# Attention and MLP on one core: two tiles in one QK tree, a new tile order, LayerNorm 1 on two engines, transposes from SBUF

## The chip, the cores and the metric

The kernel runs on one core of a Trainium2 chip. The metric is the device time of one execution, in microseconds (us). The times of the kernel before are 365.12, 364.94 and 365.55 us, median 365.12. The engines named below are PE (TensorE, the matrix unit, with PEld for its weight loads), DVE (VectorE), ACT (ScalarE), POOL (GpSimd) and SP (SyncE, which here only issues DMAs).

## The reference, cut to what matters

```python
def _A_ref(x, wqkv, wo):                 # 32 heads of width 18, window 8, dilation 2
    q, k, v = split(x @ wqkv)            # D = 576, S = 2048
    idx = pos[:, None] - (arange(8) * 2)[None, :]          # the token itself and 7 earlier ones
    logits = einsum("bhsd,bhswd->bhsw", q, k[idx]) * 18 ** -0.5   # -1e9 where idx < 0
    return einsum("bhsw,bhswd->bhsd", softmax(logits), v[idx]) @ wo

def _B_ref(x, w1, b1, w2, b2):           # hidden width 4608
    return gelu(layernorm(x) @ w1 + b1) @ w2 + b2

h = x + _A_ref(layernorm(x), wqkv, wo)   # LayerNorm 1
out = h + _B_ref(layernorm(h), w1, b1, w2, b2)   # LayerNorm 2 (two layernorms in a row)
```

## The kernel before, in words

Token 16p + j lies in partition p of tile j, so there are 16 tiles of 128 tokens by 576 columns. A query tile j attends to the eight tiles of its own parity. Tiles above j are needed shifted down by one partition: once such a tile's own attention is done, a shifted copy (a "halo") is read back over it from DRAM (`store_halo`, `halo`). Hence tiles attend from high to low: 14, 12, 10, ..., 0, then 15, 13, ..., 1, in pairs called groups (`GROUPS`).

The program is one order of instructions for each engine, written out by hand; nothing is rescheduled. Every queue is served in that order, and SP's too: a DMA that must wait holds all behind it. It has these stages.

- **QKV.** 24 visits (numbered 0 to 23 here) of two "duos". A duo is one tile times one of Wq, Wk, Wv: 18 matmuls of half the array (10 in a first phase, 8 in a second), accumulated in one of three rotating PSUM pairs. ACT copies each result out (`qkv_duo`, its `evac`, L312). The lists `after`, `between` and `hooks` say what is put behind, between and inside the visits. The even tiles (0, 2, 4, ... first) fill visits 0 to 11, the odd ones 12 to 23, each pair of odd tiles taking three.
- **LayerNorm 1** feeds QKV. The mean and variance of nearly all tiles come from DVE (`bn_stats`, L149). Even tiles are centred by DVE, transposed on PE (`tr_x`), copied out of PSUM, and the factor 1/deviation is applied by ACT at the eviction. Odd tiles are normalized by ACT (L175), stored to DRAM (`out_x`) and read back by a transposing DMA in pairs (`in_x`).
- **Attention.** For one tile, DVE multiplies the keys of all eight window places with q (`att_qk_a`, L342), sums 18 head columns in a tree (`att_qk_add`, L348, L355), takes the maximum (`att_max`); ACT does the exponential; DVE divides (`att_den`), multiplies with v (`att_pv_a`, L394) and sums (`att_pv_b`, L400, L401). The result is transposed: for the first two tiles on PE (`tr_o`), for the others by a store to DRAM (`dma_out`, two DMAs) and a transposing DMA (`oT`). Then 18 matmuls with Wo (`wo_duo`), and h = that + x (`ln2_h`).
- **LayerNorm 2** mostly runs on ACT (`ln2_act`, `ln2_send`, L475 to L483, L175) with the power on POOL (L478); its result goes the same way through DRAM and a transposing DMA into `hnT`. Tiles 14 and 12 take statistics on DVE and are transposed on PE (`tr_h`).
- **MLP**, for each of the eight groups, k = 0 to 7. The first half (`mlp1`) is 324 half-array matmuls with hnT as the moving operand and ends in GELUs on ACT (L557), the second (`mlp2`, or `mlp2_fast` from k = 2 on, with fewer products and DVE sums of their operands) ends in the output. In k = 0 and 1 the second half is two tiles of 36 rows each, a row being two matmuls. `ia[n]` hangs work in front of row n of the first tile, `ib[n]` of the second; `m1[v]` in front of visit v of `mlp1`. While group k is in the MLP, DVE does the attention of the next ones; the Wo matmuls and LayerNorm 2 of group k+1 come inside the second half of group k, so that its hnT is there for the next `mlp1`.

The semaphores of SP's DMAs are reused in turn by eight, so that a DMA waits for the eighth before it.

Of the kernel before, what the change touches and what calls it, by code (L numbers as in the profile page):

```python
# [8 lines left out]
ACT = mybir.ActivationFunctionType  # L9
# [8 lines left out]
def kernel(  # L18
# [49 lines left out]
    w2a_sb = wpool.tile([P, FA, D], BF16, name="w2a_sb")  # L68
# [22 lines left out]
    wqh_sb = qp.tile([P, 3, HALF], BF16, name="wqh_sb")  # L91

# [19 lines left out]
    def load_wqkv(t, k0=0, k1=KF):  # L112
        load(wq_sb[:, k0:k1, t * D:(t + 1) * D],
             A_wqkv[k0 * P:k1 * P, t * D:(t + 1) * D].rearrange("(k p) c -> p k c", p=P))

    def load_wqkv_half(engine, t, r):
        c0 = t * D + r * HALF
        engine.dma_start(out=wqh_sb[half_rows(r), t, :], in_=A_wqkv[KF * P:D, c0:c0 + HALF])

    def load_wo(qs):  # L120
        src = A_wo.rearrange("(h d) c -> h d c", h=H)
        for q in qs:
            load(wo_sb[q * H:(q + 1) * H, :, :], src[:, q:4 * KF:4, :])
            load(woh_sb[q * H:(q + 1) * H, :], src[:, 4 * KF + q % 2, q // 2 * HALF:(q // 2 + 1) * HALF])

    def load_w1h():
        load(b1_bf[:], B_b1.rearrange("(ft p) -> ft p", p=P))
        src = B_w1[KF * P:D, :].rearrange("p (u g c) -> p u g c", u=NU, g=2)
# [3 lines left out]
    def load_w1(c):  # L132
        cols = slice(c * F // 6, (c + 1) * F // 6)
        load(w1_sb[:, :, cols], B_w1[0:KF * P, cols].rearrange("(k p) c -> p k c", p=P))
# [7 lines left out]
    def ln_stats(srcs, tag, c1, c0, bufs, first=None, eps=True):  # L142
        n = len(srcs)
        pool = qp if tag.startswith("ln1") else sb
        stats = pool.tile([P, n, 2, nc.vector.BN_STATS_DIM], F32, tag=f"{tag}_stats", name=f"{tag}_stats", bufs=bufs)
        mv = pool.tile([P, n, nc.vector.BN_AGGR_DIM], F32, tag=f"{tag}_mv", name=f"{tag}_mv", bufs=bufs)
        for i, src in enumerate(srcs):
# [3 lines left out]
            if i == 0 and first is not None:  # L151
                first()
        if not eps:
            return mv, None
# [23 lines left out]
    def transpose_in(pt, src, tail=None):  # L178
        for kt in range(KT):
            c = min(kt * P, D - P)  # L180
            if kt < KF or tail is None:
                nc.tensor.transpose(pt[:, kt, :], src[:, c:c + P], ident[:])  # L182
        if tail is not None:
            nc.tensor.transpose(pt[:, KF, :], tail[:].rearrange("p r c -> p (r c)"), ident[:])
            return
        nc.tensor.transpose(pt[0:HP, KF, :], src[:, KF * P:D], ident[:])


    stored = [None]

    def dma_out(src):
        td = dram.tile([P, KT * P], BF16, tag="td", name="td", bufs=4)
        nc.sync.dma_start(out=td[:, 0:D], in_=src)
        stored[0] = nc.sync.dma_start(out=td[:, D:KT * P], in_=src[:, KF * P:D]).ins
        return td

    def dma_transpose(dst, src):
        td = dma_out(src)
        nc.sync.dma_start_transpose(out=dst, in_=td[:])
# [9 lines left out]

    def phase(duo, swap, after):  # L210
        first = last = None
        n = len(duo["g"][0])
        for i in range(n):
            for kt in range(KF if swap else KT):
                for r in range(2):
                    lhsT, rhs = duo["op"](r ^ swap, i, half_rows(r), kt)
# [36 lines left out]
    xnT, xn_tail = {}, {}  # L253
# [7 lines left out]
    def tr_x(js, tag):  # L261
# [12 lines left out]
        for copy in copies:  # L274
            copy()
# [817 lines left out]
```

## Time and profile before

| | |
|---|---|
| times | 365.12, 364.94, 365.55 us |
| span of the profiled execution | 364.9 us (no separate time of that execution is given; the times lie 0.0 to 0.7 above the span) |
| granted TensorE clock | 1.000 |
| first matmul of QKV | 6.26 us |
| first matmul of `mlp1` in k = 0, k = 1 | 71.05 us, 109.22 us |
| end of the first half of k = 5, k = 6 | 273.93 us (256.14 + 17.79), 310.10 us (292.31 + 17.79) |
| PE busy in 39.69-71.05, 71.05-109.22, 109.22-147.03 us | 31.36 of 31.36, 38.17 of 38.17, 37.81 of 37.81 us |
| DVE busy in the same stretches | 28.71, 35.98, 35.63 us |
| PE busy in 147.03 us to the end | 214.12 of 217.9 us |

Busy time of an engine only counts where that engine is the last to be waited for. The chain that ended last and the waits tell that; the timeline gives the order on one engine, with the duration of one instruction and what it had waited for. For DMAs, SP's line gives the time its queue needs to issue one, and "to landing" the time from the start of the issue until the data are there.

### The profile page before, as it was taken

The page shows a single profiled execution, that of the slowest core. Times are in us where ns is not written, and L with a number is a line of the kernel's source. Part 1 is how long each engine was busy: PE and PEld are TensorE (multiplying, and loading weights), DVE is VectorE, ACT ScalarE, POOL GpSimd, SP SyncE. Part 2 cuts the span into 40 slices and gives each one's busy share as a digit, 9 for nine tenths or more (in the row PEclk, how much of TensorE's full clock was granted, in tenths as well). Part 3 has the DMA queues.
Part 4 walks back from the last instruction along what each step waited for, and adds up shares of the span by engine and source line. Part 5 has one row for each costly group of instructions (what it writes and reads, how often), then busy time and mean ns, then how long its engine had stood idle before and what let it go on. Part 6 is the DMA issues. An engine that isn't in the chain of part 4 may idle for free.

```text
span 364.9 us, 11410 instructions
## 1 busy us (share of the span) xinstructions
PE 357.1 (98%) x4891; PEld 291.4 (80%) x4891; DVE 302.3 (83%) x422; ACT 229.2 (63%) x507; POOL 37.1 (10%) x47
## 2 busy tenths in 40 slices
PE   8999799999999999999999999999999999999996
PEld 5678687788778878887888778877887788778874
DVE  5899989999899998999899989998799999710431
ACT  4779655799555684468646954695469366805630
POOL 2141003000111020101010211020101100100000
PEclk9999999999999999999999999999999999999999
DMA  7979998984436743531353155503642342120001
GB/s 226 300 153 330 239 238 184 359 286 73 136 103 88 178 178 77 82 110 51 85 121 88 37 131 91 87 35 92 131 64 59 74 84 72 37 56 19 2 2 33
DMA packets 61907, 43.70 MB, mean 120 GB/s; under 512 B 31888, under 2 KB 60176, under 8 KB 61856
## 3 DMA queue, kind: packets, MB, share of 16 engines
q1 hardware_dynamic: 59968, 41.13, 42.2%
q0 software_dynamic: 1728, 1.77, 4.6%
q8 instruction: 38, 0.62, 0.7%
q10 hardware_dynamic: 160, 0.07, 0.1%
q14 instruction: 13, 0.11, 0.1%
HBM read 21.10 MB, written 12.42 MB: 92 GB/s over the span
## 4 chain that ended last, share of the span: by engine, by line
PE 92%; DMA 5%; SPq 1%; ACT 1%; issue 0%; DVE 0%
PE pm L217 38%; PE po L664 26%; PE pq L217 12%; PE po L576 10%; PE pw L217 5%; DMA oT<-td 2%; DMA wq_sb<-in_A_wqkv_dram 1%; DMA xnT<-xd 1%; DMA xd<-q_all 1%; SPq L104 1%; PE xt_pt L182 1%; ACT kv_ring L312 0%; PE h_pt L182 0%; PE o_pt L182 0%; ACT q_all L175 0%
## 5 line engine op out<-in xcount | busy, mean ns | idle before, releaser
L557 ACT ACTIVATE h_all<-pm,b_sb 128x256 f16<-128x256 f32 (+1 forms) x288 | 108.5, 497 | 69.7 <-PE pm L217 69.7
L217 PE MATMUL pm<-hnT,w_sb 64*128 64x256 bf16 x2304 | 143.0, 269 | 0.0
L217 PEld LDWEIGHTS <-w_sb 64*128 64x128 bf16 x2304 | 111.8, 94 | 15.0 <-issue 1.7
L664 PEld LDWEIGHTS <-h_all 128*128 128x128 f16 x512 | 49.4, 98 | 14.0 <-issue 1.6
L217 PE MATMUL pq<-wq_sb,xnT 64*128 64x288 bf16 x768 | 54.7, 283 | 3.1 <-DMA xnT<-xd 2.2
L217 PEld LDWEIGHTS <-xnT 64*128 64x128 bf16 x864 | 43.1, 94 | 13.0 <-DMA xnT<-xd 2.5
L348 DVE TENSOR_TENSOR prod<-prod 128x2304 bf16<-128x2304 bf16 (+1 forms) x64 | 44.2, 691 | 2.0
L394 DVE TENSOR_TENSOR prod<-kv_ring,probs 128x4608 bf16<-128x4608 bf16 x16 | 40.9, 2555 | 2.4 <-DMA kv_ring<-kv_dram 2.0
L342 DVE TENSOR_TENSOR prod<-kv_ring,q_all 128x4608 bf16<-128x4608 bf16 x16 | 40.8, 2549 | 0.5 <-DMA kv_ring<-kv_dram 0.3
L217 PE MATMUL pm<-hnT,w1h_sb 64*128 64x256 bf16 x288 | 39.2, 269 | 0.0
L664 PE MATMUL po<-w2a_sb,h_all 128*128 128x288 bf16 (+1 forms) x282 | 38.9, 286 | 0.0
L400 DVE TENSOR_TENSOR prod<-prod 128x2304 bf16<-128x2304 bf16 (+1 forms) x32 | 33.9, 1058 | 1.1
L576 PEld LDWEIGHTS <-h_all 128*128 128x128 bf16 x288 | 27.9, 98 | 7.9 <-issue 1.0
L664 PEld LDWEIGHTS <-kv_ring 128*128 128x128 f16 x252 | 24.6, 98 | 6.3
L478 POOL TENSOR_TENSOR ln_rstd<-ln_var,mhalf 128x1 f32<-128x1 f32 x13 | 12.0, 924 | 171.1 <-ACT ln_var L477 171.1
L576 PE MATMUL po<-w2a_sb,h_all 128*128 128x288 bf16 x224 | 28.5, 286 | 0.0
L664 PE MATMUL po<-w2b_sb,h_all 128*128 128x288 bf16 (+1 forms) x142 | 21.3, 286 | 0.0
L217 PE MATMUL pw<-wo_sb,oT 64*128 64x288 bf16 x256 | 19.6, 283 | 0.4 <-DMA oT<-td 0.4
L735 ACT COPY po<-po 128x288 f32<-128x288 f32 x18 | 6.9, 384 | 19.7 <-PE po L664 18.6
L644 DVE TENSOR_TENSOR kv_ring<-h_all 128x1536 f16<-128x1536 f16 (+3 forms) x9 | 6.8, 752 | 14.7 <-ACT h_all L557 14.7
L162 POOL TENSOR_TENSOR ln_rstd<-ln_veps,mhalf 128x1 f32<-128x1 f32 (+2 forms) x14 | 13.4, 967 | 50.3 <-DVE ln_veps L156 34.7
L217 PEld LDWEIGHTS <-oT 64*128 64x128 bf16 x288 | 13.6, 94 | 5.0 <-DMA oT<-td 1.2
(110 smaller groups left out, 387.3 us busy)
## 6 DMA issues: line engine op xcount, KB each, us to landing
w_sb<-in_B_w_dram SPq DMA_DIRECT2D x6, 768.0 KB, 5.9
kv_ring<-kv_dram SPq DMA_DIRECT2D x28, 144.0 KB, 2.8
w2a_sb<-in_B_w_dram SPq DMA_DIRECT2D x4, 1008.0 KB, 6.2
kv_dram<-kv_ring SPq DMA_DIRECT2D x13, 288.0 KB, 3.3
out_dram<-o_sb SPq DMA_DIRECT2D x15, 144.0 KB, 2.6
td<-q_all SPq DMA_DIRECT2D x14, 144.0 KB, 1.8
td<-hn SPq DMA_DIRECT2D x14, 144.0 KB, 1.8
x_all<-in_A_x_dram SPq DMA_DIRECT2D x12, 144.0 KB, 2.9
```

The costliest lines, as they stand in the source:

```text
L162: nc.gpsimd.tensor_tensor(out=rstd[:], in0=veps[:], in1=mhalf[:].to_broadcast([P, n]), op=ALU.pow)
L217: last = nc.tensor.matmul(duo["g"][r ^ swap][i], lhsT=lhsT, rhs=rhs, start=(swap == 0 and i == 0 and kt == 0), stop=(swap == 1 and kt == K ...
L342: nc.vector.tensor_tensor(out=prod[:], in0=k_ring[j % 2], in1=q_all[:, j, :].unsqueeze(1) .to_broadcast([P, W, D]), op=ALU.mult)
L348: nc.vector.tensor_tensor(out=prod[:, :, o * H:o * H + n], in0=prod[:, :, a * H:a * H + n], in1=prod[:, :, c * H:c * H + n], op=ALU.add)
L394: nc.vector.tensor_tensor(out=prod[:].rearrange("p w (d h) -> p w d h", h=H), in0=v_ring[j % 2].rearrange("p w (d h) -> p w d h", h=H), in ...
L400: nc.vector.tensor_tensor(out=prod[:, 0:n, :], in0=prod[:, 0:n, :], in1=prod[:, n:2 * n, :], op=ALU.add)
L478: nc.gpsimd.tensor_tensor(out=rstd[:], in0=var[:], in1=mhalf[:], op=ALU.pow)
L557: pace[0] = nc.scalar.activation(out=hT(grp)[:, f, 0:N], in_=ps[:, r, i * N:(i + 1) * N], func=ACT.Gelu_apprx_tanh, bias=b1_sb[:, f:f + 1] ...
L576: nc.tensor.matmul(banks[half], lhsT=hT(grp)[:, f, i * P:(i + 1) * P], rhs=w2_rows(f)[:, half * HALF:(half + 1) * HALF], start=(f == 0), s ...
L644: nc.vector.tensor_tensor(out=s_slot(t, m0, m1), in0=a, in1=b, op=alu)
L664: nc.tensor.matmul(bank, lhsT=l, rhs=r, start=start, stop=stop, skip_group_check=True)
L735: nc.scalar.copy(out=bank[seed[step][1]], in_=bank[seed[step][0]])
```

## The change

What it does, part by part:

1. **Tile order.** QKV begins with tiles 14 and 12, the first that attend (`LN_ORDER`, called T: 14, 12, 0, 2, 4, 6, 8, 10, 1, 3, ...). The visits are now: 0 k of 14, 12; 1 k of 0, 2; 2 q of 14, 12; 3 k of 4, 6; 4 k of 8, 10; 5, 6 q of 0, 2, 4, 6; 7 to 10 v of all even tiles; 11 q of 8, 10; 12 to 23 as before. Wv is loaded later, Wk is loaded with all its parts on SP's queue.
2. **LayerNorm 1.** Nine tiles take their statistics on DVE (`ln_dve`), seven on ACT (`ln_mean`, `ln_sq`). All are centred on DVE into 640 columns (two runs of 320 that overlap), and all get 1/deviation at the eviction; POOL computes it for two or four tiles at a time (`ln_rstds`).
3. **Transposes.** Only the first four tiles of LayerNorm 1 are transposed on PE, five transposes a tile instead of six. All else is transposed by DMA directly from SBUF to SBUF: LayerNorm 1 tile by tile (`in_x`), attention output and LayerNorm 2 in one DMA for a pair of tiles (`tr_o`, `ln2_in`, tile `y`, one buffer). The stores to DRAM ahead of the transposes are gone. hnT and oT hold the pair as two tiles side by side, so the moving operand of `mlp1` is two runs of 128 columns instead of one of 256.
4. **QK.** For the first four groups of tiles (14 and 12, 10 and 8, 6 and 4, 2 and 0) the products of two tiles are summed once each (`qk_sum9`) into one array and then share one tree (`qk_tree`). For 14 and 12 the sums of PV are shared too (`pv_mul`, `pv_tree`).
5. **Order around the first groups.** Tile 12 reads its window one place lower in the ring (`kv_low`, `window`), so it does not wait for tile 14's halo to overwrite it. The Wo matmuls of 14 and 12 come together behind visit 19, their LayerNorm 2 is on DVE for both (`first_h`, `first_hn`) and by one DMA transpose. In k = 0 both Wo visits of the next group stand in front of row 22 of the second half; the exponential of tiles 10 and 8 is taken together.

The diff, cut:

```diff
+    LN_ORDER = ATT_ORDER[:2] + EVEN[:-2] + ODD
-    def dma_transpose(dst, src):
-        td = dma_out(src)
-        nc.sync.dma_start_transpose(out=dst, in_=td[:])
+    def dma_transpose(dst, src):
+        return nc.sync.dma_start_transpose(out=dst, in_=src).ins
+    def y_transpose(dst, kind, g):
+        return dma_transpose(dst.rearrange("p i k t -> p (i k) t"), y_of.pop((kind, g))[:].rearrange("p i c -> p (i c)"))
+    def in_x(*js):
+        for j in js:
+            if j not in xnT:
+                new_xnT([j, LN_ORDER[LN_ORDER.index(j) + 1]])
+            dma_transpose(xnT[j], x_wide(j))
...
-                scale = dict(scale=rstd_of[j]) if j in EVEN else {}
-                                               func=ACT.Copy, **scale).ins
+                                               func=ACT.Copy, scale=ln1_rstd[:, ln_at(j)]).ins
...
+    def qk_sum9(j, i, rows):
+        side[j] = i
+        nc.vector.tensor_tensor(out=rows[:, :, i * HALF:(i + 1) * HALF], in0=prod[:, :, 0:HALF],
+                                in1=prod[:, :, HALF:D], op=ALU.add)
+    def qk_mul(j, i, rows):
+        att_qk_a(j)
+        qk_sum9(j, i, rows)
+    def qk_tree(js, rows):
+        v = rows.rearrange("p w (i c) -> p w i c", i=2)
+        for n in (4, 2, 1):
+            nc.vector.tensor_tensor(out=v[:, :, :, 0:n * H], in0=v[:, :, :, 0:n * H],
+                                    in1=v[:, :, :, n * H:2 * n * H], op=ALU.add)
+        nc.vector.tensor_tensor(out=logits[:].rearrange("p i w h -> p w i h"), in0=v[:, :, :, 0:H],
+                                in1=v[:, :, :, 8 * H:9 * H], op=ALU.add)
...
+    def tr_o(g):
+        t = sb.tile([P, 2, KT, P], BF16, tag="oT", name="oT")
+        y_transpose(t[:], "o", g[0])
+    def ln2_in(g):
+        hnT[g] = sb.tile([P, 2, KT, P], BF16, tag="hnT", name="hnT")
+        read[0] = y_transpose(hnT[g][:], "hn", g)
...
-                return (w1_sb[sl, kt, f0:f0 + P] if kt < KF else w1h_sb[sl, c0:c0 + P]), ht[sl, kt, 0:N]
+                return (w1_sb[sl, kt, f0:f0 + P] if kt < KF else w1h_sb[sl, c0:c0 + P]), ht[sl, :, block(kt), :]
...
+        load_x(T[0:1])
+        load_x(T[1:2])
+        load_wqkv(1)
+        load_x(T[2:3])
+        load_x(T[3:4])
+        load_x(T[4:6])
+        load_x(T[6:8])
+        load_wqkv(0)
+        load_x(ODD[0:4])
...
+        def first_h():
+            for j in g0:
+                ln2_h(j)
+            apply0.append(ln2_first(g0))
+        def first_hn():
+            apply0[0]()
+            ln2_in(g0[0])
+            for j in g0:
+                put_b2(j)
...
         after = {
+            0: [c_(tr_of, 2), lambda: copies[2](0, copy_dve), lambda: copies[2](1, copy_dve), c_(ln_mean, T[5]), c_(ln_dve, T[4]),
+                c_(ln_veps, 2, 3, False), c_(ln_veps, 3, 4, True)],
+            1: [c_(ln_center, T[5]), c_(in_x, T[4], T[5]), c_(ln_dve, T[6]), c_(ln_center, T[7]), c_(in_x, T[6], T[7]), c_(ln_sq, T[5]),
+                c_(ln_veps, 4, 5, False), c_(halo_low, 1), c_(load_x, ODD[4:8]), load_v],
+            2: [c_(ln_sq, T[7]), c_(ln_dve, ODD[0]), c_(ln_veps, 5, 6, True), c_(ln_dve, ODD[1])],
+            3: [c_(ln_dve, ODD[2]), c_(ln_veps, 6, 7, False), c_(ln_veps, 7, 8, True), c_(ln_dve, ODD[3]), c_(in_x, *ODD[0:2])],
+            4: [c_(ln_veps, 8, 12, False), c_(qk_mul, A[0], 0, first_rows), c_(qk_mul, A[1], 1, first_rows), load_small],
+            5: [c_(ln_rstds, 8, 12), c_(halo, A[0], 1)],
            6: [c_(ln_mean, ODD[5]), c_(qk_tree, A[0:2], first_rows), c_(att_max, A[0:2]), c_(load_wo, range(2))],
+            7: [c_(ln_mean, ODD[6]), c_(load_wo, range(2, 4)), c_(halo, A[1], 1)],
            8: [c_(ln_mean, ODD[7]), c_(ln_dve, ODD[4]), c_(in_x, *ODD[2:4])],
+            9: [c_(ln_sq, ODD[5]), c_(ln_center, ODD[5]), c_(halo_low, 2)],
            10: [c_(ln_sq, ODD[6]), c_(ln_center, ODD[6]), c_(ln_center, ODD[7])],
            11: [c_(ln_sq, ODD[7]), c_(att_den, *A[0:2]), c_(pv_mul, A[0], 0, first_rows), c_(ln_veps, 12, 13, False), c_(in_x, *ODD[4:6])],
+            12: [c_(pv_mul, A[1], 1, first_rows), c_(ln_veps, 13, 16, True), c_(ln_rstds, 12, 16)],
+            14: [c_(in_x, *ODD[6:8])],
            15: [c_(halo, A[0], 2), c_(halo, A[1], 2), c_(pv_tree, A[0:2], first_rows), c_(tr_o, g0)],
+            17: [c_(qk_mul, A[2], 0, odd_rows)],
+            18: [c_(halo, A[2], 1)],
+            19: [c_(att_qk_a, A[3]), c_(wo_visit, (A[0], "D"), (A[1], None)), first_h, c_(qk_sum9, A[3], 1, odd_rows)],
+            21: [first_hn, c_(halo, A[3], 1), c_(qk_tree, A[2:4], odd_rows), c_(att_max, A[2:4])],
         }
         between = {
+            1: [c_(ln_mean, T[7])],
+            11: [c_(att_exp, *A[0:2])],
...
         hooks = {
+            0: {2: c_(ln_rstds, 0, 2)},
+            1: {2: c_(ln_rstds, 2, 4)},
+            3: {2: c_(ln_rstds, 4, 6)},
+            4: {2: c_(ln_rstds, 6, 8)},
...
+        ln_dve(T[0])
+        ln_mean(T[1])
+        ln_center(T[1])
+        tr_of(0)
+        copies[0](0, copy_act, (0, 2, KT))
+        copies[0](1, copy_dve)
+        ln_sq(T[1])
+        ln_mean(T[3])
+        ln_sq(T[3])
+        ln_dve(T[2])
+        ln_center(T[3])
+        ln_veps(0, 1, False)
+        ln_veps(1, 2, True)
...
             if k == 0:
-                m1[0] += [c_(halos, 1), c_(load_w2, 4), c_(att_qk_a, d), c_(att_qk_rest, d, 1), c_(halo, d, 1)]
-                mid[0] = {1: [c_(exps, d)]}
-                m1[1] = [c_(pv_t, c), c_(pv_t, d), c_(att_qk_a, e), c_(halo, e, 1)]
-                late_wo = wo_duo(c, "B")
-                ia[0] = [c_(ln2_h, c), c_(ln2_act, c), c_(put_b2, c), c_(ln2_send, c), c_(att_qk_rest, e, 0)]
-                ia[19] = [lambda d=d: wo_visit((d, "A"), fill=True), c_(ln2_h, d), c_(ln2_act, d), c_(put_b2, d), c_(att_qk_a, f),
-                          c_(halos, 2), c_(halo, f, 1), c_(ln2_send, d), c_(ln2_ins, c, d), c_(att_qk_rest, f, 1), c_(exps, e, f)]
-                ib[0] = [c_(finish_out, g[0]), c_(att_den, e, f), c_(pv_sum, e), c_(send_o, e)]
+                m1[0] += [c_(halos, 1), c_(load_w2, 1), c_(load_w2, 2)]
+                mid[0] = {1: [c_(exps, c, d)]}
+                m1[1] = [c_(accumulate_hs, *g), c_(qk_mul, e, 0, odd_rows), c_(halo, e, 1), c_(att_den, c, d), c_(pv_sum, c), c_(load_w2, 3), c_(pv_sum, d), c_(tr_o, GROUPS[1])]
+                m1[2] = [c_(load_w2, 4)]
+                ia[0] = [c_(halos, 2), c_(qk_mul, f, 1, odd_rows), c_(halo, f, 1)]
+                ia[22] = [c_(wo_visit, (c, "B"), (d, "C")), c_(ln2_pair, c, d), c_(qk_tree, (e, f), odd_rows), c_(att_max, (e, f)), c_(exps, e, f)]
...
             if 2 < k < 7:
-                m1[0] += [c_(pv_sum, c), c_(send_o, c), c_(pv_sum, d), c_(read_o, c), c_(send_o, d), c_(read_o, d)]
+                m1[0] += [c_(pv_sum, c), c_(pv_sum, d), c_(tr_o, GROUPS[k + 1])]
```

## The prediction

> **What bounds the kernel now.** I read the page first (engines, slices, chain), then the waits, then the chain in order of time, and last the timeline of DVE, ACT and SP around the places where the change moves work.
>
> The page's engine table and slices:
>
> ```profile
> PE 357.1 (98%) x4891; PEld 291.4 (80%) x4891; DVE 302.3 (83%) x422; ACT 229.2 (63%) x507; POOL 37.1 (10%) x47
> PE   8999799999999999999999999999999999999996
> DVE  5899989999899998999899989998799999710431
> ```
>
> PE is busy throughout but for the start, one slice in QKV and the end. DVE is nearly as full until slice 32, so work that PE awaits from DVE has little room. The waits of PE and PEld (total us, times, longest):
>
> ```profile
> PEld L217 <- DMA xnT<-xd: 2.5, 1, 2.5
> PE pq L217 <- DMA xnT<-xd: 2.2, 1, 2.2
> PEld L217 <- DMA oT<-td: 1.2, 3, 0.5
> PE pw L217 <- DMA oT<-td: 0.4, 2, 0.2
> ```
>
> Only 2.2 us (first odd tiles) and two waits of 0.2 us (oT in k = 5 and 6) are PE's own. The chain shows them, and the transposes that PE does itself:
>
> ```profile
> 10.36 0.39 PE xt_pt L182 x5
> 10.74 0.17 PE xt_pt L186
> ...
> 34.32 5.33 DMA xnT<-xd
> ...
> 271.90 2.81 DMA oT<-td
> ...
> 308.14 2.74 DMA oT<-td
> ```
>
> The durations used below stand in the timeline:
>
> ```profile
> 25.93 2.55 DVE L342 TENSOR_TENSOR prod<-kv_ring,q_all 128x4608 bf16<-128x4608 bf16 x1
> 26.04 3.00 POOL L162 TENSOR_TENSOR ln_rstd<-ln_veps,mhalf 128x2 f32<-128x2 f32 x1 [1.47 <-DVE ln_nmr L171]
> ...
> 60.09 1.35 DVE L348 TENSOR_TENSOR prod<-prod 128x2304 bf16<-128x2304 bf16 x1
> ...
> 78.66 0.42 ACT L380 ACTIVATE logits<-logits 128x256 f32<-128x256 f32 x1
> ...
> 103.60 2.54 SPq L493 DMA_TRANSPOSE hnT<-td  x2
> ```
>
> POOL's power, 0.70 us when alone, ended 0.56 us after the DVE product beside it: I let it end so wherever DVE runs a wide sum.
>
> **What PE gains at most.** Before, ten tiles are transposed on PE inside QKV after the start: seven at 0.56 us, three at 0.39 us, 5.1 us. After, two at 0.39 us: 4.3 us less. The 2.2 us wait goes too, since odd tiles are centred by 22 us and needed at 37. If nothing else waited, the first `mlp1` would begin 5.5 us earlier. The rest of the working asks what is late instead.
>
> **The unknown: a transpose out of SBUF.** No row shows one. The nearest rows: one tile from DRAM lands in 2.8 us (hnT, range 2.8-3.5) or 3.8 us (oT, 2.7-4.9), a pair (xnT) in 4.8 us (3.8-5.3) under heavy loads. Two hnT transposes in a row, a pair's bytes under light load, take 1.25 + 2.9 = 4.2 us. I take 4.2 us for a pair (call it L) and 3.8 us, with 1.25 us of SP, for a single tile. Low end of L: 3.1 us, the fastest pair less 0.7 us, which is what a copy from SBUF (b2, 2.1 us) gains on one from DRAM (the halo, 2.8 us) of the same size. High end: 6.1 us, two of the slowest single ones (1.2 + 4.9).
> [...]
>
> **Visits 0 to 4.** The third tile's x lands at 7.42 us as before, the fourth I put at 8.0. ACT now does the fourth's mean and square (0.8 + 0.9) ahead of the first eviction, and the power for the first tiles waits for the fourth's centring: eviction at 10.4 instead of 8.79 us. The second duo of visit 1 needs that PSUM pair, so visit 1 ends at 12.8, visit 2 (same wait, one eviction on) at 15.5. Tiles 4 to 10 are centred by DVE at 12.1, 13.0, 14.5 and 15.1; their transposes follow in SP's queue at 12.2, 13.45, 14.7, 15.9 and land 3.8 later, the second at 17.25 and the fourth at 19.7. So visit 3 ends at 19.0 and visit 5 begins at 21.4. Before it began at 22.0 (39.69 less the 2.22 wait and seven visits of 2.205). Bounds, by singles at 2.9 and 4.9: 20.9 and 22.5. Wv, 1.3 MB behind these transposes on SP, is in by 24 and needed at 25.8. ACT's load (two evictions 1.37 + one mean or square 0.85 in a visit of 2.2) is that of before (1.37 + 0.86).
>
> **From there to the first `mlp1`, DVE sets the time.** It starts tile 14's product when the last k is evicted (22.65). Two products and sums 2 x (2.55 + 1.36), shared tree 1.22 + 0.69 + 0.42 + 0.69 (2048 wide by the slope of the rows), maximum 1.73, one LayerNorm tile 1.5, three centrings 1.2, division 2.3, two PV products and sums 2 x (2.56 + 1.36), shared sums 2.2; with 0.03 a step it ends at 50.8. oT lands at 55.0; PE has ended visit 19 at 54.5, waits 0.5 and finishes Wo at 57.2. DVE goes on: product of tile 10 to 53.4, reload of its halo 2.8 (row: 2.0 to 10.1) to 56.2, product of tile 8 to 58.8, and only then, because it is queued behind, h twice (1.5) to 60.3, statistics and aggregates 2.2 + 0.15 to 62.7, POOL beside the 1.36 sum to 64.6, two scalings to 66.1 (0.75 each as other f32 rows; 0.45 as the lower end), transpose L to 70.3. PE has the four visits done at 66.0 and stands 4.3 us. `mlp1` begins at 70.3, before at 71.05: **-0.75 us**. The shared trees save 0.64 us a pair (3.19 x 2 against 2 x 1.36 + 3.02), which is in this. Of the 5.5 us, 4.8 are lost on this chain.
>
> **Group k = 0.** Before it took 38.17 us; without stalls PE needs 17.79 + 2.2 + 17.75 = 37.74. The exponential of both tiles now stands where one stood, 7.6 us in, and ends at 8.25. Before, DVE divided the other tile meanwhile (74.86); now, with tile 6's product and sum done, it idles for some 4 us. Then 2.3 of division, 5.2 of PV (2.56 + 1.36 + 0.76 + 0.49) for the first tile; the second's waits for the v halo, reloaded after the first's product (13.2 + 2.8 to 3.6), begins at 16.4 and ends at 21.6. Transpose: 21.7 + L = 25.9. PE is at row 22 at 17.79 + 22 x 0.2466 = 23.2 and waits **2.7 us**. The last W2 load (w2b, queued on SP behind this transpose) lands some 5 to 7 us after 23.3 and is needed six rows past Wo, at 29.6: I take 0.3. LayerNorm 2 of both tiles ends 6.9 us after Wo (ACT 2 x 2.0, POOL 0.75, ACT 2 x 1.2, DVE's h before them); 6.9 + 4.2 = 11.1 fits the 12.3 us of rows left. Sum 40.7 against 38.17: **+2.55 us**.
>
> **k = 1 to 7.** In k = 1 Wo stands at the head of the second half; DVE ends the PV of its pair some 10 us into the group, so L hides behind 17.79. From k = 3 on the pair is one transpose after the second tile's PV, instead of two stores (1.9 us to land, 0.76 of issue) and a transpose. DVE ends that 12.9 us into k = 5 and 13.8 into k = 6; plus L: 17.1 and 18.0 against 17.79. Before 0.2 + 0.2, after 0 + 0.2: **-0.2 us**. The one-buffer tile y makes PV's last sum wait for the hnT transpose; that is issued 5 us or more before `mlp1` begins. Fewer SP issues (28 transposes for 32, no 64 stores) lie beside other work. ACT's scale on odd evictions (+0.09 each) lies in its idle time of some 0.7 us a visit. The moving operand in two runs: 2592 matmuls at 0.0549 us (17.79 / 324), those of QKV 0.0613 (8.83 / 144). Per column that is 0.214 and 0.213 ns for 256 and 288, so columns alone seem to count and I take nothing; nothing hides it, and eight columns' time a matmul would be 4.4 us. A gain is excluded, the columns being as many.
>
> **Sum.** 364.9 - 0.75 + 2.55 - 0.2 = 366.5 for the span; the median of the runs lies 0.2 above the span, so **366.7 us**. A microsecond of L counts twice, at the first hnT and at row 22.
>
> **Rivals.**
> - *The SBUF transpose lands fast.* SP's stores and DRAM's latency are gone, and the copies of b2 (2.1 us) speak for it. At L = 3.1 the two places give 2.2 us back; with halos at their 2.0 us 0.8 more: 363.7. It decides for "faster" from L below 3.3. Against it: a pair never landed under 3.8.
> - *It lands slowly, or SP issues it long.* At L = 5.3, the slowest pair: +2.2, k = 5 and 6 +1.5, single tiles at 4.9 +0.5: about 371. For it speaks that singles spread to 4.9 under load, and that tiles 4 to 10 queue behind 590 KB of x.
> - *The split moving operand costs PE.* +4.4 at the bound: 371. Against it: columns alone set the two rows that exist.
>
> **Chances.** The sum 0.42 (its own range 365 to 369), fast 0.33, slow 0.18, split 0.07. 0.2% is 0.73 us, about what a measurement of this kernel can tell from no change. Faster takes most of the fast case and a little of the sum's: 0.31; same, from the edges of both, 0.12; slower 0.57. The range runs from the fast case with its small terms (362.8) to the slow one (372).
>
> **What would show it.** Right: PE stands before the first `mlp1` for hnT by DMA (about 4 us) and before Wo in k = 0 (about 3 us), DVE idles some 4 us in k = 0 until the exponential, visit 5 begins near 21.4. Wrong: hnT there at the end of visit 23, a pair landing below 3.3 us or above 5, matmuls of `mlp1` longer than 0.055 us apart, or stalls in visits 5 to 18, which I have at none.

## The result, and the profile after

The changed kernel takes 377.27 us (median; 376.47 to 378.03), the kernel before beside it 365.03: a ratio of 1.0335, 95% interval 1.0312 to 1.0359. Forecast were 366.7 us and at most 372.0. Of the 10.6 us that the forecast missed, 7.9 lie inside the profiled span (374.4 against 366.5), and 1.9 because the time lies 2.1 us above the span in this kernel, not 0.2; the last 0.8 are between the profiled execution and the median.

The page of the changed kernel, engine table and slices:

```profile
PE 354.1 (95%) x4842; PEld 296.8 (79%) x4842; DVE 295.1 (79%) x375; ACT 225.7 (60%) x509; POOL 34.4 (9%) x43
PE   8899369989889999999999999999999999999996
...
PEclk9999769999999999999999999999999999999999
DMA  7999896387675372250271235323421322110001
```

PE falls to 3 and 6 tenths in the fifth and sixth slice (37 to 56 us), and there, and only there, the granted clock falls too. The waits of PE and PEld (total, times, longest):

```profile
PEld L240 <- POOLq L250: 9.9, 1, 9.9
PE pq L240 <- POOLq L250: 9.6, 1, 9.6
PE pw L240 <- DMA oT<-o: 2.1, 2, 1.2
PE po L593 <- DMA w2b_sb<-in_B_w_dram: 1.3, 1, 1.3
```

The second line is new: one wait of 9.6 us, for the POOL instruction of L250, more than PE's other waits together (7.4 us). That line is `marker`, the empty POOL instruction that lets the second phase of a half's visit begin. The timeline tells what held it, and what came after:

```profile
49.69 0.16 DVE L814 TENSOR_SCALAR ln_veps<-ln_mv 128x3 f32<-128x3 f32 x1
...
49.93 2.10 POOL L818 TENSOR_TENSOR ln_rstd<-ln_veps,mhalf 128x4 f32<-128x4 f32 x1 [24.20 <-DVE ln_veps L814]
...
49.97 3.06 PE L240 MATMUL pq<-wq_sb,xnT 64*128 64x288 bf16 x24 [9.56 <-POOLq L250]
...
58.47 1.60 SPq L203 DMA_TRANSPOSE oT<-o  x1
60.17 0.53 SPq L352 DMA_DIRECT2D w_kv<-kv_dram  x1
...
63.43 2.56 DVE L368 TENSOR_TENSOR prod<-w_kv,q_all 128x4608 bf16<-128x4608 bf16 x1 [7.54 <-DMA w_kv<-kv_dram]
...
74.16 1.36 SPq L203 DMA_TRANSPOSE hnT<-hn  x1
...
77.86 0.61 PE L240 MATMUL pm<-hnT,w_sb 64*128 64x256 bf16 x8 [0.98 <-ACT q_all L325]
```

`ln_rstds(12, 16)`, the power for the last four odd tiles, stands on POOL behind visit 12. Its operand is a 0.16 us DVE instruction that stands behind the PV products of tiles 14 and 12 and is done at 49.85. The markers of visit 13 come later in POOL's queue, so PE stood from 40.4 to 49.97. DVE, for its part, stood 7.5 us at tile 8's product for the reload of the halo. The first `mlp1` begins at 77.86 us instead of 71.05 (+6.8); PE had then just ended its own late visits and waited 0.98 us for ACT's last eviction. The first matmul of k = 1 comes at 118.77 (in the chain below its piece begins at 118.84), so k = 0 takes 40.91 us (38.17 before, +2.7), and from the start of k = 2 on the two kernels need the same (217.8 and 217.9).

The chain of k = 0:

```profile
85.52 0.64 ACT logits L415
...
99.19 1.36 SPq L203
...
100.65 7.20 DMA w2b_sb<-in_B_w_dram
...
118.84 17.79 PE pm L240 x324
```

### The profile page after: what moved, and what is told of

Same layout as the page of the kernel before. It is cut to its first block, busy times and chain, and to the rows that moved or that the text cites. A ratio compares the mean times of both kernels' runs of the same rounds, so it can differ in the third digit from the quotient of the medians.

```text
span 374.4 us, 11202 instructions
## 1 busy us (share of the span) xinstructions
PE 354.1 (95%) x4842; PEld 296.8 (79%) x4842; DVE 295.1 (79%) x375; ACT 225.7 (60%) x509; POOL 34.4 (9%) x43
## 4 chain that ended last, share of the span: by engine, by line
PE 69%; DVE 4%; DMA 3%; ACT 2%; issue 1%; SPq 0%
PE pm L240 32%; PE po L681 26%; PE po L593 8%; PE pw L240 4%; DMA w2b_sb<-in_B_w_dram 2%; DVE prod L425 1%; DMA oT<-o 1%; DVE prod L431 1%; ACT h_all L574 1%; SPq L203 0%; ACT L415 0%; ACT L550 0%; DVE den L419 0%; DVE o L432 0%; DVE probs L421 0%
## 5 line engine op out<-in xcount | busy, mean ns | idle before, releaser
L681 PE MATMUL po<-w_kv,h_all 128*128 128x288 bf16 (+1 forms) x366 | 49.7, 286 | 0.0
L431 DVE TENSOR_TENSOR prod<-prod 128x2304 bf16<-128x2304 bf16 (+1 forms) x28 | 29.6, 1058 | 1.0
L368 DVE TENSOR_TENSOR prod<-w_kv,q_all 128x4608 bf16<-128x4608 bf16 x8 | 20.5, 2557 | 11.1 <-DMA w_kv<-kv_dram 9.5
L593 PE MATMUL po<-w_kv,h_all 128*128 128x288 bf16 x224 | 28.3, 286 | 0.0
L681 PEld LDWEIGHTS <-w_kv 128*128 128x128 f16 x216 | 21.1, 98 | 5.4
L374 DVE TENSOR_TENSOR prod<-prod 128x2304 bf16<-128x2304 bf16 (+3 forms) x32 | 22.1, 691 | 1.1
L425 DVE TENSOR_TENSOR prod<-w_kv,probs 128x4608 bf16<-128x4608 bf16 x8 | 20.4, 2556 | 2.0 <-DMA w_kv<-kv_dram 1.8
L368 DVE TENSOR_TENSOR prod<-kv_ring,q_all 128x4608 bf16<-128x4608 bf16 x8 | 20.4, 2556 | 0.1
L325 ACT ACTIVATE q_all<-pq,ln_rstd 128x576 bf16<-128x576 f32 x16 | 11.5, 736 | 15.1 <-PE pq L240 15.0
L425 DVE TENSOR_TENSOR prod<-kv_ring,probs 128x4608 bf16<-128x4608 bf16 x8 | 20.4, 2553 | 0.1
```

What stands on the lines that cost most here:

```text
L325: pace[0] = nc.scalar.activation(out=dst.rearrange("p (d g h) -> p g d h", g=2, h=H // 2), in_=ps[:, :, 0:HALF].rearrange("p g (h d) -> p ...
L368: nc.vector.tensor_tensor(out=prod[:], in0=window(j, 1), in1=q_all[:, j, :].unsqueeze(1) .to_broadcast([P, W, D]), op=ALU.mult)
L374: nc.vector.tensor_tensor(out=prod[:, :, o * H:o * H + n], in0=prod[:, :, a * H:a * H + n], in1=prod[:, :, c * H:c * H + n], op=ALU.add)
L425: nc.vector.tensor_tensor(out=prod[:].rearrange("p w (d h) -> p w d h", h=H), in0=window(j, 2).rearrange("p w (d h) -> p w d h", h=H), in1 ...
L431: nc.vector.tensor_tensor(out=prod[:, 0:n, :], in0=prod[:, 0:n, :], in1=prod[:, n:2 * n, :], op=ALU.add)
L593: nc.tensor.matmul(banks[half], lhsT=hT(grp)[:, f, i * P:(i + 1) * P], rhs=w2_rows(f)[:, half * HALF:(half + 1) * HALF], start=(f == 0), s ...
```

## Experiments

Two stalls, then, before the first `mlp1`: PE's for POOL, and DVE's for a transfer. Every kernel below is compared with the kernel before on the same chip; "start" is the start of the first `mlp1`, "k = 0" the time from there to that of k = 1.

| run | ratio to before (95%) | start | k = 0 |
|---|---|---|---|
| changed kernel | 1.0335 (1.0312 to 1.0359) | 77.86 | 40.9 |
| e1_power_late | 1.0301 (1.0246 to 1.0357) | 77.49 | 40.9 |
| e2_variance_early | 1.0317 (1.0238 to 1.0395) | 76.06 | 40.8 |
| b1_pool_waits (kernel before) | 1.0272 (1.0216 to 1.0327) | 78.48 | 38.2 |
| e3_w1_late | 1.0159 (1.0124 to 1.0194) | 70.23 | 42.2 |
| e7_w1_late_only | 1.0409 (1.0395 to 1.0423) | 79.12 | 43.0 |
| e4_odd_pairs | 1.0299 (1.0273 to 1.0324) | 75.87 | 40.7 |
| e11_two_loads_late | 1.0208 (1.0180 to 1.0237) | 72.92 | 40.7 |
| e5_h_first | 1.0129 (1.0098 to 1.0159) | 69.35 | 41.6 |
| e6_exp_early | 1.0236 (1.0219 to 1.0253) | 78.55 | 38.6 |
| e8_all_moves | 1.0302 (1.0286 to 1.0317) | 68.92 | 47.8 |
| e9_wo_loads_later | 1.0317 (1.0299 to 1.0336) | 72.08 | 46.6 |
| e10_w2_behind_halo | 1.0110 (1.0093 to 1.0127) | 69.04 | 39.4 |
| e12_two_loads_exp | 1.0142 (1.0098 to 1.0186) | 73.28 | 38.7 |

**POOL's wait taken away, in two ways.** The power moved, or its operand made earlier:

```diff
e1:
-            12: [c_(pv_mul, A[1], 1, first_rows), c_(ln_veps, 13, 16, True), c_(ln_rstds, 12, 16)],
+            12: [c_(pv_mul, A[1], 1, first_rows), c_(ln_veps, 13, 16, True)],
...
-            17: [c_(qk_mul, A[2], 0, odd_rows)],
+            17: [c_(ln_rstds, 12, 16), c_(qk_mul, A[2], 0, odd_rows)],
e2:
-            11: [..., c_(pv_mul, A[0], 0, first_rows), c_(ln_veps, 12, 13, False), c_(in_x, *ODD[4:6])],
+            11: [..., c_(ln_veps, 12, 13, False), c_(ln_veps, 13, 16, True), c_(pv_mul, A[0], 0, first_rows), c_(in_x, *ODD[4:6])],
-            12: [c_(pv_mul, A[1], 1, first_rows), c_(ln_veps, 13, 16, True), c_(ln_rstds, 12, 16)],
+            12: [c_(pv_mul, A[1], 1, first_rows), c_(ln_rstds, 12, 16)],
```

> The changed kernel with one instruction moved: POOL's power for the last four odd tiles stands behind visit 17 instead of behind visit 12. Theory A (the markers of visit 13 queue on POOL behind a power that waits for DVE, and PE stands for them): PE's 9.6 us stall goes, the granted clock stays at full, the first mlp1 is at 70 to 71 us instead of 77.9 (DVE's chain sets it: last product of tile 8 at about 60, h 61.6, hn 66.7, transpose 3.4), k = 0 stays at 41 us; span 367, 7 to 8 us under the changed kernel. Rival B (the stall only covers a later wait, DVE behind the reload of the halo, which stood 7.5 us): the first mlp1 moves by less than 3 us, to 75 or later, span 372 or more. Rival C (the power's own 2 to 3 us beside a wide DVE instruction hold the markers, wherever it stands): 2 us or more of PE's wait for POOL are left in visit 18.

> The changed kernel with one DVE instruction moved: the variances of the last three odd tiles (0.16 us) stand ahead of tile 14's PV product instead of behind tile 12's; POOL's power stays behind visit 12. Theory A (what holds the markers is that the power waits for its operand): the operand is there at 40 us, PE's wait for POOL falls from 9.6 us to under 1, the clock stays at full, the time is that of the run with the power moved, within 0.7 us. Rival C (the power's duration holds the markers): PE waits until the power ends, 2 to 3 us in visit 13, and the time is 2 to 3 us above that of the other run. Rival B: no gain beyond 3 us against the changed kernel.

PE's wait for POOL was gone in both, and the start moved by 0.4 and 1.8 us only; the ratios are not distinguishable from that of the changed kernel. My theory A, that the stall's 9.6 us were the loss, fell: rival B held. Other waits took its place: in e2 PE stood 2.9 us for odd tiles (xnT) and 4.5 us for oT, and after that wait it ran at half clock for some 3 us (eight matmuls in 1.14 us instead of 0.66). The timeline of e2:

```profile
40.15 3.24 POOL L818 TENSOR_TENSOR ln_rstd<-ln_veps,mhalf 128x4 f32<-128x4 f32 x1 [14.41 <-DVE ln_veps L814]
...
40.19 1.65 PE L240 MATMUL pq<-wq_sb,xnT 64*128 64x288 bf16 x24
...
51.20 0.83 DVE L445 TENSOR_TENSOR o<-w_kv 128x1280 bf16<-128x1280 bf16 x1
...
53.83 0.53 SPq L111 DMA_DIRECT2D w_sb<-in_B_w_dram  x1
...
55.45 1.51 SPq L203 DMA_TRANSPOSE oT<-o  x1
57.06 0.52 SPq L352 DMA_DIRECT2D w_kv<-kv_dram  x1
...
62.35 1.14 PE L240 MATMUL pw<-wo_sb,oT 64*128 64x288 bf16 x8 [4.53 <-DMA oT<-o]
...
62.84 2.56 DVE L368 TENSOR_TENSOR prod<-w_kv,q_all 128x4608 bf16<-128x4608 bf16 x1 [6.95 <-DMA w_kv<-kv_dram]
```

The attention result is ready at 52.0, but its transpose is issued at 55.45 (two single transposes, a w1 load and two halos are ahead of it on SP), and it lands 6.9 us later. The halo, issued at 57.06, lands at 62.8. Rival C fell too: the power ran 3.2 us from 40.15 and PE went on at 40.19, as in the changed kernel it went on 0.04 us after the power began (49.93 and 49.97). What held the markers here is the waiting of the power at the head of POOL's queue, not its run time.

**The same stall put into the kernel before.**

```diff
-            11: [c_(out_x, 2)],
+            11: [c_(out_x, 2), pool_waits],
...
+        def pool_waits():
+            nc.gpsimd.tensor_tensor(out=scratch[:], in0=q_all[:, A[0], 0:1], in1=mhalf[:], op=ALU.mult)
```

> The kernel before with one more instruction: POOL, behind visit 11, multiplies one column of tile 14's attention result, which DVE has ready at 47.1 us. Nothing uses the product. Theory A: the markers of visit 12 queue behind it, PE stands from 40.9 to 47.1 us, 6.2 us, the granted clock falls to about half behind it for some 4 us (1 to 1.4 us more), and the first mlp1 is 6 to 8 us later: span 371 to 373. Rival D (PE's stall in the changed kernel comes from elsewhere, a DMA or DVE, and POOL's order costs nothing): 365, as before. Without the clock's part: 371. This run also shows how time and span stand to one another outside the changed kernel.

```profile
46.07 0.19 POOL L892 TENSOR_TENSOR scratch<-q_all,mhalf 128x1 f32<-128x1 bf16 x1 [17.85 <-DVE q_all L401]
...
46.13 3.06 PE L217 MATMUL pq<-wq_sb,xnT 64*128 64x288 bf16 x24 [7.65 <-POOLq L227]
...
49.23 1.17 PE L217 MATMUL pq<-wq_sb,xnT 64*128 64x288 bf16 x8
```

One POOL instruction of 0.19 us costs the kernel before 9 to 10 us: 7.65 of waiting, and some 2 because the clock is at half until about 50.7 (eight matmuls take 1.17 us there and 0.65 later). Theory A held (span 372.3, 371 to 373 given) and rival D fell: the mechanism is real and had its full price here, where nothing was late beside it. Why had it none in the changed kernel? From 38 to 61 us the DMA engines are fuller than in the kernel before. That stretch in the kernel before (length, busy time and count of PE, PEld, DVE, ACT and POOL, the granted clock, the busy share of the DMA engines, GB/s):

```profile
38.00:61.00 23.00, 21.31 (x339) 17.91 (x341) 21.02 (x29) 12.85 (x23) 2.80 (x1) 1.00 0.97 236
```

and in e2:

```profile
38.00:61.00 23.00, 16.88 (x269) 12.97 (x263) 15.74 (x13) 11.95 (x20) 3.24 (x1) 1.00 1.07 275
```

**The transfers taken out of the way,** on top of e2:

```diff
-        loads = {v: [c_(load_w1, c)] for c, v in enumerate((6, 7, 9, 10, 12, 14))}
-        loads[19] = [c_(load_w2, 0)]
+        loads = {6: [c_(load_w1, 0)], 7: [c_(load_w1, 1)], 18: [c_(load_w1, 2), c_(load_w1, 3)],
+                 19: [c_(load_w1, 4), c_(load_w1, 5)]}
...
-                m1[0] += [c_(halos, 1), c_(load_w2, 1), c_(load_w2, 2)]
+                m1[0] += [c_(halos, 1), c_(load_w2, 0), c_(load_w2, 1), c_(load_w2, 2)]
```

> The run with the early variances, and the last four of the six loads of w1 (0.77 MB each) moved from behind visits 9, 10, 12, 14 to behind visits 18 and 19, the first load of w2 from behind visit 19 to the start of k = 0. Theory E (SP's queue and the DMA engines are full from 38 to 61 us, so that the transpose of tiles 14 and 12 is issued 3 to 4 us after its operand is ready and lands 7 us later, and the halo that DVE's product of tile 8 waits for lands at 62.8): the transpose is issued at about 52.6 and lands by 57, the halo by 59, PE's waits for xnT go, the first mlp1 comes at 70 to 72 us instead of 76.1, the time falls by 4 to 6 us to 369 to 371. Rival F (a transpose out of SBUF takes 7 us there whatever else runs): oT lands at 59.5 or later, the first mlp1 at 73.5 or later, a gain under 3 us.

```profile
52.08 1.44 SPq L203 DMA_TRANSPOSE oT<-o  x1
...
57.73 2.56 DVE L368 TENSOR_TENSOR prod<-w_kv,q_all 128x4608 bf16<-128x4608 bf16 x1 [1.82 <-DMA w_kv<-kv_dram]
...
70.23 0.61 PE L240 MATMUL pm<-hnT,w_sb 64*128 64x256 bf16 x8 [1.76 <-DMA hnT<-hn]
```

Theory E held: oT was issued at once and landed in 5.2 us, the halo by 57.7, 0.7 us of PE's wait for xnT was left, and the start came at 70.23 us, 5.8 earlier than in e2. The price is 1.4 us more in k = 0: the wait for w2b (1.2 us) is gone, but PE waits 2.3 us for oT instead of 1.2, and after that wait the clock falls to half for about 3 us (lines in the last section).

**The same move with POOL's wait left in.** The edit of e3 on the changed kernel itself:

> The changed kernel with the loads of w1 and w2 moved as in the run with w1 late, but POOL's power and the variances left where the change put them. Theory K (PE's stall behind POOL and the transfers behind SP are two waits beside each other; each hides the other): PE stands 9.5 us in visit 13 as in the changed kernel, ends QKV only at 77, the first mlp1 is at 77 to 78.5 us and the time 375.5 to 378.5, no gain worth the name, though the same move gained 5.5 us where POOL's wait was gone. Rival (the two costs add): the first mlp1 at 72 to 73, the time 371 to 373.

```profile
49.99 3.06 PE L240 MATMUL pq<-wq_sb,xnT 64*128 64x288 bf16 x24 [8.92 <-POOLq L250]
...
79.12 0.61 PE L240 MATMUL pm<-hnT,w_sb 64*128 64x256 bf16 x8 [0.98 <-ACT q_all L325]
```

Theory K held, its start and time a little above what it gave: no gain, even 1.3 us of loss at the start (the clock stayed low until about 55.5 us here, and until 53 in the changed kernel), and 2.1 us more in k = 0, where PE stood 3.1 us for oT. So each cause alone brings the start to 76 us or later: the transfers alone to 76.1 to 77.5 (e2, e1), the stall alone to 79.1 (e7). Both together make 77.9, and without both it is 70.2.

**SP's time or the DMA engines'?** In e4 the odd tiles are centred side by side, in rows of w2's buffer that are still free, and four transposes of a pair replace eight of a tile:

```diff
-            return kv_ring[1][:, j // 2, :, :].rearrange("p t d -> p (t d)")[:, 0:WIDE]
+            n = ODD.index(j)
+            return w2_kv[:, 12 * D + n * WIDE:12 * D + (n + 1) * WIDE]
...
+        if js[0] in ODD:
+            for a, b in zip(js[::2], js[1::2]):
...
+                n = ODD.index(a)
+                dma_transpose(t[:].rearrange("p i k t -> p (i k) t"), w2_kv[:, 12 * D + n * WIDE:12 * D + (n + 2) * WIDE])
```

> The run with the early variances, and the eight odd tiles centred side by side in rows of w2's buffer that are still free, so that four transposes of a pair take the place of eight of a tile; the loads stand where they stood. Theory E, with SP's issue time the tighter of the two: some 5 us of SP's time are gone (eight issues of 1.3 against four of 1.35), oT is issued at 52.6 instead of 55.5, the first mlp1 comes 2 to 4 us earlier, at 72 to 74. With the DMA engines the tighter: oT is issued earlier but lands no more than 1 us earlier, the first mlp1 at 75 to 76. Rival G (a single transpose is slower to land than a pair, by the tile's place in the key and value rows): xnT lands in under 4 us and PE's two waits for xnT (1.3 and 1.6 us) go, but the first mlp1 does not move.

```profile
54.15 2.68 SPq L203 DMA_TRANSPOSE oT<-o  x1
```

```profile
62.02 0.66 PE L241 MATMUL pw<-wo_sb,oT 64*128 64x288 bf16 x8 [4.17 <-DMA oT<-o]
```

oT was issued 1.3 us earlier (54.15), but landed at 62.0 instead of 62.35, and the start moved 0.2 us: the DMA engines (a share of 1.06 from 38 to 61 us) are the tighter. In e11 only the two w1 loads just ahead of oT were moved (c = 4 and 5, to visit 18):

> The run with the early variances, and only the last two loads of w1 (0.77 MB each, issued there at 49.2 and 53.8 us, just ahead of oT and the halo) moved behind visit 18; the other loads stand where the change put them. Theory E, narrowed to these two: oT is issued by 53 us and lands by 58, the halo by 60, the first mlp1 at 70 to 72 us as in the run with four loads late, k = 0 stays at 41 us: time 368.5 to 370.5. Rival L (the stage as a whole is short of transfer time, all loads count): the odd transposes still queue behind the loads issued at 42 to 45 us, the first mlp1 at 73 or later, time 371.5 or more.

The start came at 72.92, between e2 and e3: with the loads issued at 42 to 45 us left in place, PE still stood 2.99 us for xnT, oT was issued only at 55.67, and the halo came at 60.5. Rival L was right, its start (73 or later) within 0.1 us and its time with 371.59: the other loads of this stretch count too.

**DVE's order.** On top of e3, h and its statistics ahead of tile 8's product:

```diff
-            19: [c_(att_qk_a, A[3]), c_(wo_visit, (A[0], "D"), (A[1], None)), first_h, c_(qk_sum9, A[3], 1, odd_rows)],
-            21: [first_hn, c_(halo, A[3], 1), ...],
+            19: [c_(wo_visit, (A[0], "D"), (A[1], None)), first_h],
+            21: [first_hn, c_(qk_mul, A[3], 1, odd_rows), c_(halo, A[3], 1), ...],
```

> The run with w1 late, and on DVE h, its statistics and the scaling of tiles 14 and 12 ahead of tile 8's product and sum, which follow the scaling. Theory H (behind the transfers the first LayerNorm 2 is held by tile 8's product, which waits for the halo, in front of h): the first mlp1 comes 2 us or more earlier than in the run with w1 late, at 67 to 69 us; then PE's own work (visits end at 66) or the transpose is the last. Rival: oT, not the halo, is last, and h was ready to go anyway: less than 1 us earlier.

0.9 us earlier, not 2: the rival's number held, but for another reason. hnT was then there in time and PE's own visits ended last (PE's last wait, 0.98 us, was for ACT's eviction). The ratios of e3 and e5 are not distinguishable.

**k = 0.** On top of e2, `exps(*GROUPS[1])` in place of the first `gelu_table()`, and `load_w2(4)` ahead of `pv_sum(d)`:

> The run with the early variances, and in k = 0 alone: the exponential of tiles 10 and 8 ahead of the first GELU table instead of behind the first visit of mlp1, and the last load of w2 ahead of the second tile's PV on SP instead of behind the transpose. Theory (k = 0 lasts 41 us because oT at row 22 and then w2b are late): PE's waits for oT in k = 0 and for w2b go, k = 0 lasts 37.7 to 38.5 us, the time falls by 2.5 to 3.3 us. Rival (DVE's own work sets oT): DVE gains only its 2.8 us of idling, and 1 us or more of the wait for oT is left.

```profile
102.43 0.67 PE L240 MATMUL pw<-wo_sb,oT 64*128 64x288 bf16 x8 [0.52 <-DMA oT<-o]
```

k = 0 fell from 40.8 to 38.55 us, with 0.5 us of wait for oT and none for w2b. (This profiled execution had a late start, with waits of 3.4 and 3.5 us before the first `mlp1`; the time of the kernel is 1.0236 of before, against 1.0317 for e2.) The two waits are nearly the whole cost of k = 0.

**All together.** e8 joins e2, e3, e5 and e6, with the last two w2 loads at the head of the second visit and tile 6's product behind the PV; e9 adds `load_wo(range(2, 4))` moved behind `halo_low(2)`; e10 is e8 with those w2 loads behind tile 10's v halo; e12 joins e11 and e6.

> All moves together: variances early, w1 late, h first, the exponential ahead of the first GELU table; and in k = 0 the last two loads of w2 at the head of the second visit, tile 6's product behind the PV of tiles 10 and 8, the first load of w2 behind hnT. If the waits named are the whole cost of the change: first mlp1 at 69 to 69.5 us, k = 0 37.8 to 38.5 us, span 362.5 to 363.5, time 364.2 to 365.5, within 0.4% of the kernel before. If something else in the change costs PE time, the span stays above 365.

```profile
90.70 2.56 DVE L425 TENSOR_TENSOR prod<-w_kv,probs 128x4608 bf16<-128x4608 bf16 x1 [8.62 <-DMA w_kv<-kv_dram]
...
99.41 1.14 PE L240 MATMUL pw<-wo_sb,oT 64*128 64x288 bf16 x8 [6.12 <-DMA oT<-o]
```

A miss, by the mechanism under study: with two w2 loads (2.2 MB) ahead of it, a halo of 0.14 MB, issued at 80.87 us, was there only for DVE's product at 90.70, 9.8 us later; in e10, where the loads stand behind it, the product came 4.4 us after the issue (79.51 and 83.95). DVE waited 8.6 us for it in e8, and k = 0 took 8.4 us longer than in e10.

> The same with half of the loads of Wo (six DMAs) behind the reload of tile 14's v halo instead of ahead of it on SP. Theory E: DVE's wait of 1.2 to 1.9 us before tile 12's PV product goes, oT is issued 1.2 us earlier, PE's wait of 1.2 us for it goes: first mlp1 at 68 to 68.3 us, time 1 us below the run with all moves. Rival: the DMA engines, not SP, hold that halo: less than 0.4 us.

A miss as well: PE's wait for oT was 3.0 us instead of 1.6, and from about 59 to 62.4 us behind it PE ran at about half its rate (16 matmuls with Wo took 2.13 us there, 1.16 in the changed kernel at 66.90), so the start came 3.2 us later than in e8. Why oT came later is not shown.

> The run with all moves, with the last two loads of w2 (1.0 MB and 1.2 MB) behind the reload of tile 10's v halo on SP instead of at the head of the second visit. In the run with all moves that halo landed 8.6 us late behind them, and oT 6.1 us late for PE. Theory E: the halo lands at 82 to 83 us, oT of tiles 10 and 8 by 92, PE waits under 1 us for it, k = 0 lasts 37.8 to 39.5 us after a first mlp1 at 69 to 69.5: span 362.5 to 365, time 364.5 to 367, 8 to 10 us under the run with all moves and within 1% of the kernel before. Rival (another cost in k = 0, the GELUs behind the exponential): PE waits for ACT or the clock stays low, span 367 or more.

> The same, and in k = 0 the exponential ahead of the first GELU table and the last load of w2 ahead of the second tile's PV. If the first mlp1 comes at 70 to 72 us and k = 0 lasts 38 to 39 us as in the run with the exponential early, the span is 364 to 366 us and the time 365.8 to 368, within 1.1% of the kernel before and the best version with the change's own order of DVE. If the changes do not add, because loads and halos meet in k = 0 again, the time is 368 or more.

e10 did what theory E gave for the start (69.04) and for k = 0 (39.4 us, without a wait for oT), but its time, 368.02, is 1 us above the forecast: 1.7 us went in k = 1 to a PE wait for DVE's output sum (`o_sb`), which DVE reached only behind the PV of another tile. e12 came out at 368.78, the side on which the changes do not add: its k = 0 has 38.7 us, but its start was late (73.28), with 2.95 us of PE waiting for xnT. e10 and e5 are the best: 1.011 and 1.013 of before. No version that I made beats the kernel before. Against the second profile of that kernel (below), e10's span is 2.9 us longer: its start is 0.4 us earlier, k = 0 takes 1.3 us more and k = 1 some 1.9 us more; what would remove these stays open.

**The kernel before, a second time.**

> The kernel before, unchanged, for a second profile. The first profiled execution has a span of 364.9 us, the timed runs of the same kernel beside the experiments have 362.0 to 362.3, with 1.7 to 1.8 us outside. Theory: the first profile caught an execution in which the pair of odd tiles came 2.2 us late; here the span is 362 to 362.5, PE has no wait for xnT over 0.5 us, the first mlp1 is at 68.2 to 68.9 us. Rival: the profile itself makes the execution longer; then span and waits are those of the first one.

```profile
44.69 0.66 PE L217 MATMUL pq<-wq_sb,xnT 64*128 64x288 bf16 x8 [0.61 <-DMA xnT<-xd]
...
69.41 0.60 PE L217 MATMUL pm<-hnT,w_sb 64*128 64x256 bf16 x8
```

Here the wait for the odd tiles is 0.61 us, not 2.22, the start 69.41, not 71.05, the span 362.8 and the time 364.59: a little above what I gave, but far from the rival's 364.9. The runs of the kernel before beside the experiments mostly have spans of 361.4 to 362.8, so the first profile had caught a late execution. Against this second profile the changed kernel's first `mlp1` comes 8.5 us later, not 6.8.

## Why the prediction was wrong, step by step

- *"stalls in visits 5 to 18, which I have at none"* is the first step that failed. I moved `ln_rstds(12, 16)` in my working only as work (a power ending "0.56 us after the DVE product beside it"), not as a wait in POOL's queue. The question "what is queued behind it, and who waits for that" had the answer: visit 13's markers, then PE. b1 shows the step by itself (9 to 10 us), e7 shows that the stall alone sets the start at 79 us.
- *"From there to the first `mlp1`, DVE sets the time"*: the chain was right and its transfers were mis-sized, so that the term of the sum forecast at -0.75 us measured +6.8. Predicted 70.3 us; e3, with neither the stall nor the crowd of loads, has 70.23, in part by luck: there the halo came 1.5 us later than I had it, and the last transpose took 3.4 us instead of 4.2. In the changed kernel's own order of loads "oT lands at 55.0" and "reload of its halo 2.8 (row: 2.0 to 10.1)" were wrong by some 7 us: in e2 they landed at 62.3 and 62.8. I took a median where the row itself reached 10.1, and did not write out SP's queue at that place. The stretches of the first profile would have shown it: from 38 to 61 us the DMA engines are 0.97 busy before (5.4 MB); e2 has 1.07 and 6.3 MB there. The halo then took 5.8 us from issue, and waited 2.5 us for its issue.
- *What PE gains at most.* The two parts, 4.3 and 2.2 us, make 6.5 and not 5.5; the forecast does not rest on this sum. Of it, 2.2 were a wait of one profiled execution (0.61 in the second). Against the second profile the repaired start of e3 is 0.8 us later than before, not 0.8 earlier.
- *"The median of the runs lies 0.2 above the span"*: each run whose span is listed lies 1.7 to 2.3 us above it, those of the kernel before 1.7 to 1.9. The first profile's 364.9 was a late execution; set against times of others, its 0.2 was an accident.
- *Group k = 0* was right in sum, +2.7 against +2.55, by parts that made up for each other: oT made PE wait 1.2 us (2.7 predicted) and w2b 1.3 (0.3). e6, which removes both, has 38.55 against 38.17 before. The w2b load, queued on SP behind the transpose, took 7.2 us and landed 30.0 us into the group; I had it at 28.3 to 30.3.
- *k = 1 to 7* was right: -0.1 against -0.2.
- *The unknown, L*: in the changed kernel hnT pairs land in 3.4 us (3.4 to 4.0), oT pairs in 4.0 (3.4 to 5.1), SP needs 1.35 us for one (1.30 to 1.79; 2.68 among the loads in e4); 4.2 was a fair price without crowding, and a long issue by SP did not show. Single tiles took 2.6 to 7.6 us against 3.8. The slow rival ("singles spread", L of 5.3) was right in kind, late transfers under load, and too small: 371. Above it my range had no case, because none joined the loads to the halo.
- *The split moving operand* costs nothing: the 324 matmuls of `mlp1` take 17.79 us in both kernels. *Visits 0 to 4*: visit 5 began at 21.7 (37.12 less seven visits of 2.205), predicted 21.4.

## What to carry to other kernels

An instruction that does nothing but signal still stood in a queue here (POOL's; 7.65 us of waiting on PE in b1, where the instruction ahead of it ran 0.19 us): for each instruction moved onto an engine, write down when its operand is ready and which signals are behind it. Where a stage shows one large stall, look for what is late beside it before pricing the stall: here a wait of 9.6 us on PE and one of 7.5 us on DVE hid one another, and removing either alone gained 1.8 us at the start at most. A halo of 0.14 MB was used 9.8 us after its issue behind two large loads (e8) and 4.4 us after it ahead of them (e10), so price a small transfer on the critical path by a row from the same stage with the same loads around it, and give a row's maximum a case of its own.

## What the runs showed of the hardware that I had not expected

**The clock after a stall.** Stretches of the changed kernel (length, then busy time and count of PE, PEld, DVE, ACT and POOL, the granted clock, the share of the DMA engines, GB/s):

```profile
44.00:47.00 3.00, 0.00 (x0) 0.00 (x0) 1.18 (x1) 0.00 (x0) 0.00 (x0) 0.50 1.12 311
...
50.00:52.00 2.00, 2.00 (x18) 1.32 (x20) 1.97 (x3) 0.74 (x1) 2.00 (x1) 0.50 1.14 283
52.00:54.00 2.00, 2.00 (x29) 1.44 (x27) 2.00 (x2) 0.83 (x2) 0.03 (x1) 0.74 1.12 339
```

PE resumed at 49.97 at half clock and had the full one again some 3 us later (1.00 in 54 to 56 us); an estimate from the two rows, 2 x 0.5 + 2 x 0.26, is 1.5 us lost. In e7, after a stall of 8.9 us, the clock stayed at half until about 55.5 us (0.50, 0.50 and 0.60 in the stretches of 2 us from 50 to 56, then 1.00); in b1, after 7.65 us, until about 50.7, 4.6 us after the restart (0.50 in 47 to 49 us, 0.56 in 49 to 51, then 1.00). Two waits of 3 us went different ways: 2.95 us in e12 were followed by eight matmuls in 1.14 us, 2.99 us in e11 by eight in 0.66.

```profile
53.49 1.14 PE L240 MATMUL pq<-wq_sb,xnT 64*128 64x288 bf16 x8 [2.95 <-DMA xnT<-kv_ring]
```

```profile
54.15 0.66 PE L240 MATMUL pq<-wq_sb,xnT 64*128 64x288 bf16 x8 [2.99 <-DMA xnT<-kv_ring]
```

In k = 0 of e3 the fall came after the wait was over: PE waited 2.29 us for oT, the next eight matmuls took 0.66 us, and only then did the granted clock fall, to a mean of 0.54 from 97 to 100 us:

```profile
96.14 0.66 PE L240 MATMUL pw<-wo_sb,oT 64*128 64x288 bf16 x8 [2.29 <-DMA oT<-o]
```

```profile
97.00:100.00 3.00, 3.00 (x28) 1.72 (x23) 1.08 (x2) 0.49 (x1) 0.00 (x0) 0.54 0.99 292
```

After the waits of 2.22 us in the kernel before and 2.65 us in e1 it did not fall (the next two times eight matmuls took 0.66 and 0.65 us in both). What decides whether the clock falls after a wait of 2 to 3 us, and what makes the way back 3 us in one run and 5.5 in another, was not shown.

**The same busy share of the DMA engines at very different byte rates.** Two stretches of e3. In the first nearly nothing but transposes of odd tiles was in flight (the two stores issued ahead of them from 43.26 us on took 3.5 us to land in the median, the next reload was issued at 50.77); the second is mostly loads of w1:

```profile
48.00:50.00 2.00, 2.00 (x36) 1.59 (x34) 1.93 (x3) 1.17 (x3) 0.00 (x0) 1.00 0.97 97
...
58.00:64.00 6.00, 6.00 (x102) 4.95 (x98) 5.90 (x11) 1.77 (x3) 0.20 (x1) 1.00 1.01 403
```

The busy share is 0.97 and 1.01, at 97 and 403 GB/s. A byte budget alone would have called the first stretch free. An estimate from these two rows (0.97 / 97 against 1.01 / 403) gives the transposes of single tiles four times the engine time per byte of the weight loads; no run varied this by itself.
